# Long convolution and expert layer: the convolution in four passes of 32 channels, with the data as matmul weights in the 90-point stage and its result kept in SBUF

## The chip, the core and the metric

One core of one Trainium2 chip runs the whole program. The metric is the device time of one execution in microseconds (us). TensorE is called PE, VectorE DVE, ScalarE ACT, GpSimd POOL; SP is the engine whose queue issues nearly all DMA transfers of this kernel.

## The reference

A batch of 4 sequences of 12,480 positions and 128 channels is multiplied by a second input, convolved along the sequence with a filter that a small MLP makes, gated, and sent through a two-layer expert with a squared ReLU. All of it is float32.

```python
h_filt = (np.maximum(pos_emb @ w1, 0.0) @ w2) * np.exp(-0.01 * pos)[:, None]
u = x * v
Uf = np.fft.rfft(u, n=2 * S, axis=1)
Hf = np.fft.rfft(h_filt, n=2 * S, axis=0)
y = np.fft.irfft(Uf * Hf[None], n=2 * S, axis=1)[:, :S, :]
t = (x * y).reshape(B * S, D)
r = np.maximum(t @ w_in, 0.0)          # 128 -> 2048
out = (r * r) @ w_out                  # 2048 -> 128
```

## The kernel before

The sequence is folded into 98 rows by 128 points. The convolution is done by matmuls with constant tables in three stages, the third of which also runs the expert.

**90-point stage** (lines 110 to 302, `conv_moe`). A group g holds four of the 128 points (two and their mirror images), all 4 batches and 128 channels. `load1` brings x and v (98 rows), `u_mul` multiplies them (one half on DVE, one on POOL, line 151), `u_eo` makes sums and differences of the mirrored points (line 159). `s1_u` multiplies with the table `e_sb` as weights: 98 rows in, 90 frequencies out, 512 moving columns, cosine and sine (line 186). ACT copies the PSUM tile to `stage` (line 195) and SP stores it to the DRAM buffer `bd` (line 213). The filter goes beside it, one group of four points at a time: `pt` is loaded, `mlp1` and `mlp2` make the filter values `ft` (lines 141, 143, 168, 170), `f_eo` their sums and differences `feo` on POOL (line 181), `s1_f` transforms and stores them too (line 208). `weights` splits a piece of the expert's weights, given as 64-bit floats, into a high and a low part straight into the SBUF tiles `wi` and `wo` (lines 250 to 270). The loop over 32 groups in line 284 sets the order on every engine by hand. The stores of the last two groups are held back in part (`late`).

**128-point stage** (lines 333 to 400). For each of the 90 frequencies k, `load2` reads a row of `bd` as `bt` (128 points by 1280 columns: data and filter) and its table `wt`. `s2` transforms the filter (line 352, 256 columns) and the data (line 357, two products of 512). DVE multiplies the two spectra (`t`, line 361), POOL adds the parts (`y`, lines 369 and 370). `i2` transforms back two rows later (line 377), ACT and DVE join the halves (`ci`, `cs`, lines 379 to 382), and SP stores the row to the DRAM buffer `cd` (line 383).

**Third stage** (lines 405 to 522). For each of the 128 points, `ca` and `cb` are read from `cd`, transformed back over the 90 frequencies (`psy`, line 434), multiplied by x, transposed, and sent through the expert in blocks of 1024 tokens (lines 461 to 493).

SP issues its DMAs strictly in the order of the program: one that waits for data holds up all that follow it. Each engine, too, takes its instructions in order.

Of the kernel before, what the change touches and what calls it, by code (L numbers as in the profile page):

```python
# [29 lines left out]
F32 = mybir.dt.float32  # L31
# [9 lines left out]
FO = 64  # L41
DFF = 2048
# [12 lines left out]
ROW = 2 * W + 2 * D  # L55
RF = -(-int(np.count_nonzero(np.exp(-0.01 * np.arange(S, dtype=np.float32)))) // N2)

TERMS = ((0, 0), (1, 0), (0, 1))


def _group(n2):

    j = n2 - H2 if n2 >= H2 else H2 - 1 - n2
    return j // 2, j % 2 + (0 if n2 >= H2 else 2)
# [8 lines left out]
def conv_moe(ctx, tc, xg, vg, pos, win, w1, w2, ew, fw, ident_d, sw, iw, iw0, w_in, w_out, out):  # L73
# [11 lines left out]
    bd = dram.tile([N1, N2 + 1, ROW], F32, tag="bd", name="bd")  # L85
# [5 lines left out]
    f_sb = const.tile([N2, 2, N2], F32, tag="f", name="f_sb")  # L91
    sp.dma_start(f_sb, fw)
    ident = const.tile([R1, R1], F32, tag="id", name="ident")
    sp.dma_start(ident, ident_d)
    win_sb = const.tile([RF, N2], F32, tag="win", name="win_sb")
    sp.dma_start(win_sb, win)
# [4 lines left out]
    wi = [const.tile([D, DFF], F32R, tag=f"wi{i}", name=f"wi{i}") for i in range(2)]  # L101
    wo = [const.tile([128, NF, D], F32R, tag=f"wo{i}", name=f"wo{i}") for i in range(2)]
# [3 lines left out]
    KL = 16  # L106
    late = {NG - 2: [], NG - 1: []}
    late_pool = ctx.enter_context(ExitStack())
    lp = late_pool.enter_context(tc.tile_pool(name="late", bufs=2, side="right"))
    with ExitStack() as c1:  # L110
        io = c1.enter_context(tc.tile_pool(name="p1io", bufs=2))
        wk = c1.enter_context(tc.tile_pool(name="p1wk", bufs=2))
        psS = c1.enter_context(tc.tile_pool(name="p1s", bufs=3, space=PSUM))
        psM = c1.enter_context(tc.tile_pool(name="p1m", bufs=1, space=PSUM))
        st, sf = {}, {}

        def load1(g):
            if g >= NG:
                return
            xt = io.tile([R1, 2, 2 * W], F32, tag="x", name="xt", bufs=3)  # L120
            vt = io.tile([R1, 2, 2 * W], F32, tag="v", name="vt")
            for t, src in ((xt, xg), (vt, vg)) if g else ():
                sp.dma_start(t, src[g].rearrange("n (h w) -> n h w", h=2))
# [12 lines left out]
        def mlp1(g):  # L136
            if g >= NG:
                return
# [7 lines left out]
        def u_mul(g):  # L146
            if g >= NG:
                return
# [485 lines left out]
```

## Time and profile before

| what | value |
|---|---|
| median of 3 runs | 3200.69 us (3195.69 to 3206.71) |
| the profiled execution, its own time | 3198.17 us |
| its span, first to last instruction | 3196.2 us |
| busy share of the span | PE 96%, DVE 76%, ACT 65%, POOL 26% |
| DMA | 370.57 MB, 153956 packets, mean 116 GB/s |

A row of a group of instructions gives line, engine, operation, output and inputs with their shapes, and how many there are; then the busy time in us and the mean of one in ns; then the idle time just ahead of them and what ended it. In the order of time a row begins with its start and its duration in us, and names the idle time ahead of it in brackets. Matmuls are pipelined, and the duration of one reaches past the start of the next; how many a stretch can hold is read from the distance of two starts. A row of a stretch of time has, for each engine, busy time and the count of instructions; then the mean clock granted to TensorE, the mean busy share of the 16 DMA engines, and GB/s.

### The profile page before, as it was taken

What the parts mean: (1) busy time and instruction counts of PE and PEld (TensorE: products, weight loads), DVE (VectorE), ACT (ScalarE), POOL (GpSimd) and SP (SyncE); (2) the same over time, 40 slices, a digit from 0 to 9 for tenths busy, and PEclk for the clock granted to TensorE, in tenths of its full rate; (3) what the DMA queues carried; (4) which work ended last, traced back from release to release, by engine and by line L of the source; (5) the groups of instructions that cost most, each with busy time, mean ns of one, the idle gap of its engine ahead of it and who ended that gap; (6) DMA issues with size and microseconds to landing.
All of it is one profiled execution on the core that took longest, in us unless ns stands there. A gap on an engine that the chain in (4) does not pass through costs nothing.

```text
span 3196.2 us, 35767 instructions
## 1 busy us (share of the span) xinstructions
PE 3078.8 (96%) x12558; PEld 2239.7 (70%) x12558; DVE 2423.3 (76%) x2832; ACT 2074.8 (65%) x2453; POOL 815.7 (26%) x593
## 2 busy tenths in 40 slices
PE   8999859999699999999999999999999999999999
PEld 3343324444388888888888888888888888888888
DVE  6787738888477777777777777777777777777776
ACT  4444402222277777777777777877777777777777
POOL 3344326666212112122121211211211121121210
PEclk9999979999799999999999999999999999999999
DMA  8999749889512122112122222212221112211200
GB/s 273 307 312 308 254 153 305 297 300 296 176 51 62 54 72 58 58 52 72 55 62 58 62 61 66 58 51 59 71 59 58 58 51 74 62 53 58 63 24 19
DMA packets 153956, 370.57 MB, mean 116 GB/s; under 512 B 14841, under 2 KB 44397, under 8 KB 147701
## 3 DMA queue, kind: packets, MB, share of 16 engines
q1 hardware_dynamic: 144417, 341.80, 33.5%
q0 software_dynamic: 9360, 26.50, 3.2%
q8 instruction: 99, 1.62, 0.2%
q14 instruction: 80, 0.66, 0.1%
HBM read 236.51 MB, written 131.73 MB: 115 GB/s over the span
## 4 chain that ended last, share of the span: by engine, by line
PE 82%; DMA 13%; DVE 2%; issue 1%; SPq 1%; ACT 0%; DVEq 0%; ACTq 0%
PE psh L461 34%; PE pso L487 33%; DMA vt<-in_v_dram 9%; PE psy L434 5%; PE psx L357 4%; PE psc L377 4%; DMA wt<-in_sw_dram 3%; PE pst L449 1%; PE psh L352 1%; PE pss L186 1%; DMA cb<-cd 0%; DVE cv L252 0%; DVE u L159 0%; SPq L383 0%; DVE xt L151 0%
## 5 line engine op out<-in xcount | busy, mean ns | idle before, releaser
L81 DVE TENSOR_TENSOR glo<-gt,ghi 128x1024 fp32r<-128x1024 f32 (+1 forms) x784 | 1087.5, 1387 | 60.8 <-DVE ghi L473 1.8
L464 ACT ACTIVATE rt<-psh 128x1024 f32<-128x1024 f32 (+1 forms) x784 | 801.8, 1023 | 387.4 <-PE psh L461 373.0
L473 DVE CAST ghi<-gt 128x1024 fp32r<-128x1024 f32 (+1 forms) x784 | 540.0, 689 | 456.1 <-ACT gt L471 453.9
L487 PE MATMUL pso<-ghi,wo 128*128 128x512 f32 (+1 forms) x3136 | 852.2, 388 | 0.0
L461 PE MATMUL psh<-xhi,wi 128*128 128x512 f32 (+1 forms) x3136 | 852.2, 393 | 0.0
L471 ACT ACTIVATE gt<-rt 128x1024 f32<-128x1024 f32 (+1 forms) x784 | 828.9, 1057 | 23.4
L487 PEld LDWEIGHTS pso<-ghi,wo 128*128 128x128 f32 x3136 | 587.8, 188 | 121.5 <-DVE os L492 0.6
L461 PEld LDWEIGHTS psh<-xhi,wi 128*128 128x128 f32 x3136 | 580.1, 188 | 117.5 <-ACT rt L464 0.4
L81 POOL TENSOR_TENSOR clo<-ca,chi 128x512 fp32r<-128x512 f32 x124 | 227.2, 1833 | 1337.0 <-ACT chi L78 1294.2
L487 PE MATMUL pso<-glo,wo 128*128 128x512 f32 (+1 forms) x1568 | 497.8, 388 | 0.0
L461 PE MATMUL psh<-xlo,wi 128*128 128x512 f32 (+1 forms) x1568 | 482.4, 389 | 0.0
L461 PEld LDWEIGHTS psh<-xlo,wi 128*128 128x128 f32 x1568 | 294.7, 188 | 62.4
L487 PEld LDWEIGHTS pso<-glo,wo 128*128 128x128 f32 x1568 | 294.2, 188 | 60.9 <-DVE glo L81 0.3
L361 DVE TENSOR_TENSOR t<-psx,hs 128x1024 f32<-128x1024 f32 x180 | 212.0, 1220 | 103.1 <-PE psx L357 85.9
L186 PE MATMUL pss<-u,e_sb 98*90 98x512 f32 x512 | 247.7, 629 | 14.5 <-DVE u L159 14.4
L379 ACT COPY ci<-psc 128x512 f32<-128x512 f32 x90 | 52.8, 586 | 297.5 <-issue 203.6
L195 ACT COPY stage<-pss 90x1024 f32<-90x1024 f32 x128 | 127.5, 1007 | 100.0 <-PE pss L186 51.4
L81 POOL TENSOR_TENSOR clo<-cb,chi 104x512 fp32r<-104x512 f32 x124 | 163.4, 1317 | 104.1 <-ACT chi L78 103.6
L186 PEld LDWEIGHTS pss<-u,e_sb 98*90 98x90 f32 x512 | 79.5, 165 | 150.5 <-issue 126.0
L377 PE MATMUL psc<-y,f_sb 128*128 128x512 f32 x360 | 176.7, 613 | 5.1 <-DVE cs L382 4.5
L357 PE MATMUL psx<-bt,wt 128*128 128x512 f32 x360 | 178.2, 619 | 0.0
L369 POOL TENSOR_TENSOR y<-t,t 128x512 f32<-128x512 f32 x90 | 114.7, 1274 | 217.5 <-DVE t L361 176.6
(64 smaller groups left out, 2209.1 us busy)
## 6 DMA issues: line engine op xcount, KB each, us to landing
bt<-bd SPq DMA_DIRECT2D x90, 640.0 KB
cd<-cs SPq DMA_DIRECT2D x90, 512.0 KB
bd<-stage SPq DMA_DIRECT2D x60, 720.0 KB
cb<-cd SPq DMA_DIRECT2D x126, 208.0 KB
iwt<-in_iw_dram POOLq DMA_DIRECT2D x64, 392.0 KB, 3.5
x<-in_x_dram SPq DMA_DIRECT2D x128, 196.0 KB
out_dram<-os SPq DMA_DIRECT2D x48, 512.0 KB
xt<-in_x_dram SPq DMA_DIRECT2D x31, 784.0 KB
```

Of the source, the lines that this page charges most:

```text
L81: eng.tensor_tensor(dst, src, hi.bitcast(F32), op=ALU.subtract)
L186: pe.matmul(ps[:, c], lhsT=e_sb[: u.shape[0], e + c], rhs=u, start=True, stop=True)
L195: act.copy(s["stage"][:, e, j].rearrange("p (c w) -> p c w", c=2), ps)
L357: pe.matmul(xp[:, c], lhsT=s["w"], rhs=s["b"][:, c * W : (c + 1) * W], start=True, stop=True)
L361: dve.tensor_tensor(tt, xp.rearrange("p c (b d) -> p (c b) d", b=B), s["h"][:, c : c + 1].broadcast_to([N2, 2 * B, D]), op=ALU.mult,)
L377: pe.matmul(cp[:, c], lhsT=f_sb[:, c], rhs=s["y"][:, c], start=True, stop=True)
L434: pe.matmul(yp, lhsT=lhs, rhs=rhs, start=n == 0, stop=n == len(ops) - 1)
L461: pe.matmul(ps[:, j, :n], lhsT=wi[wp][:, f * 128 : (f + 1) * 128], rhs=bl[b][dp][:, j * n : (j + 1) * n], start=(wp, dp) == TERMS[0], stop ...
L464: act.activation(rt, ps[:, :, :n], AF.Relu)
L471: act.activation(gt, rt, AF.Square)
L473: dve.tensor_copy(hi, gt)
L487: pe.matmul(un["o"][j], lhsT=wo[tm[0]][:, f], rhs=g[tm[1]][:, j], start=f == 0 and tm == TERMS[0], stop=f == NF - 1 and tm == TERMS[-1])
```

## The change

**Four passes.** The 128 channels are taken in four passes of 32 (`Q = 4`). Within a pass the 90-point and the 128-point stage follow each other; the result of the first, for all 90 frequencies, stays in one SBUF tile `P` with a single buffer. The DRAM buffer `bd` is gone. `cd` is written in pieces of 128 columns (512 bytes) where a row had 512.

**90-point stage.** A pass has 20 chunks of 8 columns: 16 of data (batch by channel) and 4 of filter. Of a data chunk, `load_c` brings x and v in one tile `xv` (three buffers), POOL multiplies all of it, DVE makes sums and differences in `u` (three buffers). In `s1_quad` the data is now the weights of the product, and the constant table `e_sb` is what moves: for each column two products of 98 rows, 64 weight columns (the sums fill PSUM partitions 0 to 63, the differences 64 to 127) and 180 moving columns. ACT copies four columns at a time into `P`.

**Filter.** All 32 groups are computed in the first 11 chunks of pass 0, three to a chunk, and stored to a DRAM buffer `fd`; the filter chunks of every pass read from it, 8 channels (32 bytes) at a time, and DVE or POOL reorders them.

**Expert weights.** They are split in 16 pieces of 256 columns, one begun at every fourth chunk as long as the pass has some left, its work spread over three chunks, and stored to the DRAM buffer `wd`; the SBUF tiles `wi` and `wo` are filled from there in the last pass.

**128-point stage.** One step `z` takes three frequencies of 32 channels (6 products of 160 columns, then `i2` with two of 384), 30 steps a pass.

The third stage has the same instructions. x is read from a copy in another order, and the first pair of points is loaded whole when the stage begins, its x and its table earlier.

The core of the diff:

```diff
-        def s1(ps, e, u):
-            for c in range(2):
-                pe.matmul(ps[:, c], lhsT=e_sb[: u.shape[0], e + c], rhs=u, start=True, stop=True)
...
-            sp.dma_start(bd[:rows, n2, : 2 * W], src[:rows])
...
+        def filt2(g):
+            h1 = sf.pop(("h", g))
+            ps = psM.tile([RF, G2, D], F32, tag="m2", name="psm2")
+            for j in range(G2):
+                pe.matmul(ps[:, j], lhsT=h1[:, j], rhs=w2_sb, start=True, stop=True)
...
+            for e, op in enumerate((ALU.add, ALU.subtract)):
+                pool.tensor_tensor(fe[:, e], ft[:, :2], ft[:, 2:], op=op)
+            sp.dma_start(fd[:, :, 2 * g : 2 * g + 2], fe)
...
+        def load_c(g):
...
+            xv = s1.tile([R1, 2, 8 * N2], F32, tag="xv", name="xv")
+            if c < NU:
+                for r in (slice(0, 96), slice(96, R1)):
+                    sp.dma_start(xv[r], xvg[q, c][r])
+            else:
+                d = q * QC + 8 * (c - NU)
+                sp.dma_start(xv[:RF, 0].rearrange("n (m s) -> n m s", s=8),
+                             fd.rearrange("n e j d -> n (e j) d")[:, :, d : d + 8])
...
+            if c < NU:
+                pool.tensor_tensor(xv[:, 0], xv[:, 0], xv[:, 1], op=ALU.mult)
+                xr = xv[:, 0].rearrange("n (h s j) -> n h s j", h=2, s=8)
+                for e, op in enumerate((ALU.add, ALU.subtract)):
+                    dve.tensor_tensor(u[:, :, e * H2 : (e + 1) * H2], xr[:, 0], xr[:, 1], op=op)
+            else:
+                (dve, pool)[c % 2].tensor_copy(u[:RF], xv[:RF, 0].rearrange("n (m s) -> n s m", s=8))
...
+            for a in range(4):
+                for e in range(2):
+                    p = slice(e * H2, (e + 1) * H2)
+                    pe.matmul(pv[p, a], lhsT=u[:rows, 4 * h + a, p],
+                              rhs=e_sb[:rows, e : e + 2].rearrange("n c k -> n (c k)"), start=True, stop=True)
+            s = 8 * c + 4 * h
+            act.copy(
+                sl["P"][:, :, s : s + 4].rearrange("p m a t -> p a m t"),
+                pv.rearrange("p a (m t) -> p a m t", t=2),
+            )
...
+            sp.dma_start(wd[i // NWP, :, :, cols].rearrange("h p c -> p h c"), st.bitcast(F32))
...
+                for c in range(NC):
+                    g = q * NC + c
+                    load_c(g + 3)
+                    for f in range(3 * c, min(3 * c + 3, NG)) if q == 0 else ():
+                        load_f(f + 2)
+                        if f + 1 < NG:
+                            filt(f + 1)
+                        filt2(f)
+                    prep(g + 2)
+                    if c % 4 == 0 and wpart < (q + 1) * 2 * NWP // Q:
+                        part = weights(wpart)
+                        wpart += 1
+                    if part and next(part, 1):
+                        part = None
+                    s1_quad(g, 0)
+                    s1_quad(g, 1)
```

**How the order moves.** On PE, in the 90-point stage of before, a group is eight products of 512 columns (a row with `x2` stands for two), the filter's transform (`feo`), and the MLP's products (`psm`):

```order
L186 MATMUL pss_221<-u_181,e_sb 90x512 x2
L186 MATMUL pss_241<-u_181,e_sb 90x512 x2
L186 MATMUL pss_247<-feo,e_sb 90x256 x4
L168 MATMUL psm_259<-w_sb,h_209 82x128 x4
L186 MATMUL pss_269<-u_183,e_sb 90x512 x2
L186 MATMUL pss_276<-u_183,e_sb 90x512 x2
L141 MATMUL psm_281<-pt,w_sb 64x328
```

On PE in the first pass after the change, one chunk of data (`pss`, line 185) follows three MLP groups (lines 128 and 137):

```order
L128 MATMUL psm_872<-pt,w_sb 64x384
L137 MATMUL psm_876<-w_sb,h_827 96x128 x4
L128 MATMUL psm_889<-pt,w_sb 64x384
L137 MATMUL psm_893<-w_sb,h_874 96x128 x4
L128 MATMUL psm_906<-pt,w_sb 64x384
L137 MATMUL psm_910<-w_sb,h_891 96x128 x4
L185 MATMUL pss<-e_sb,u 64x180 x16
```

Three MLP groups now stand ahead of each chunk's products, and each of the latter has 180 moving columns in place of 512.

On SP, a group of before has the loads of pt, x, v and a piece of raw weights, and the stores to bd:

```order
L133 DMA pt<-in_pos_dram 64x328
L123 DMA xt<-in_x_dram 98x2048
L123 DMA vt<-in_v_dram 98x2048
L237 DMA raw<-in_w_in_dram 128x256
L213 DMA bd<-stage 90x2x1024
L208 DMA bd<-fstage 90x2x256 x2
L213 DMA bd<-stage 90x2x1024
```

On SP in the first pass after the change (`wst` is a finished piece of weights, `feo` the filter's sums and differences):

```order
L232 DMA wd<-wst 128x2x256
L155 DMA xv<-in_xv_dram 96x2048
L155 DMA xv<-in_xv_dram 2x2048
L123 DMA pt<-in_pos_dram 64x384
L145 DMA fd<-feo 192x1x256
L123 DMA pt<-in_pos_dram 64x384
L145 DMA fd<-feo 192x1x256
```

Each load of pt now stands behind the store of an earlier group's feo, and the loads of xv behind the store of a piece of weights.

On SP at the end of the second pass's 90-point stage (the rows with `xv<-fd` are the filter chunks):

```order
L155 DMA xv<-in_xv_dram 96x2048
L155 DMA xv<-in_xv_dram 2x2048
L210 DMA raw<-in_w_in_dram 128x512
L158 DMA xv<-fd 96x128x8 x2
L232 DMA wd<-wst 128x2x256
L158 DMA xv<-fd 96x128x8 x2
```

The loads from fd are new; before had no access in runs of eight elements.

More of the change, by code (lines that the diff above doesn't have):

```diff
@@ new lines, in conv_moe, with load_f, filt @@
+    win_sb = const.tile([RF, N2], F32, tag="win", name="win_sb")
+    sp.dma_start(win_sb, win)
+    f_sb = const.tile([N2, 2, N2], F32, tag="f", name="f_sb")
+    ident = const.tile([R1, R1], F32, tag="id", name="ident")
+    with ExitStack() as c1:
+        big = c1.enter_context(tc.tile_pool(name="big", bufs=1))
+        right = ExitStack()
+        s1 = right.enter_context(tc.tile_pool(name="s1", bufs=3, side="right"))
+        psX = c1.enter_context(tc.tile_pool(name="psx", bufs=2, space=PSUM))
+        pro = ExitStack()
+        wf = pro.enter_context(tc.tile_pool(name="filter", bufs=2))
+        psM = pro.enter_context(tc.tile_pool(name="psm", bufs=2, space=PSUM))
+        ch, sf, sl = {}, {}, {}
+        def load_f(g):
+            if g < NG:
+                pt = wf.tile([FO, G2 * RF], F32, tag="pos", name="pt")
+                sp.dma_start(pt, pos[g])
+                sf[g] = pt
+        def filt(g):
+            ps = psM.tile([FO, G2 * RF], F32, tag="m1", name="psm1", bufs=1)
+            pe.matmul(ps, lhsT=w1_sb, rhs=sf.pop(g), start=True, stop=True)
+            h1 = wf.tile([FO, G2, RF], F32, tag="h1", name="h1")
+            act.activation(h1.rearrange("p a b -> p (a b)"), ps, AF.Relu)
+            sf["h", g] = h1
+        def filt2(g):
+            h1 = sf.pop(("h", g))
@@ new lines, in s1_quad @@
+        def s1_quad(g, h):
+            c = g % NC
+            u, rows = ch["u", g], R1 if c < NU else RF
+            ps = psX.tile([N2, 2, 512], F32, tag="x", name="pss")
+            pv = ps.rearrange("p c (a w) -> p (c a) w", a=2)[:, :, : 2 * N1]
+            for a in range(4):
[4 more added lines that the diff above has]
+            s = 8 * c + 4 * h
@@ L265, in weights_end @@
-        def weights_end():
-            if pending:
-                hi, lo, fm, fr = pending.pop()
+                yield
+                wl, wh = raw[:, :, 0], raw[:, :, 1]
+                t, sg, m, rest = (s1.tile([128, CW], U32, tag=f"cv{n}", name=f"cv{n}", bufs=1) for n in range(4))
+                shl, shr = ALU.logical_shift_left, ALU.logical_shift_right
+                dve.tensor_scalar(t, wh, 1, 21, op0=shl, op1=shr)
+                ti = t.bitcast(I32)
+                dve.tensor_scalar(ti, ti, 896, 0, op0=ALU.subtract, op1=ALU.max)
@@ new lines, in conv_moe, with load3 @@
+    io3 = ctx.enter_context(tc.tile_pool(name="p3io", bufs=2))
+    def load3(p):
+        if p not in st3:
+            load3_w(p)
+        ca = io3.tile([128, 2, W], F32, tag="ca", name="ca")
+        cb = io3.tile([2 * CB, 2, W], F32, tag="cb", name="cb")
+        re, im = (cd[p + h * H2].rearrange("(c k) w -> k c w", c=2) for h in range(2))
+        M = 128 - N1
+        sp.dma_start(ca[:N1], re)
+        sp.dma_start(ca[N1:], im[:M])
+        for q in range(2):
+            sp.dma_start(cb[q * CB : (q + 1) * CB], im[M:])
+        st3[p].update(ca=ca, cb=cb)
```

410 lines of the change are left out of this document (153 added, 257 removed).

## Prediction

> **What bounds the kernel now.** I read the page, then busy time by stage, then the order of time inside each stage. The chain that ended last is mostly TensorE, but that is an average over three stages:
>
> ```profile
> span 3196.2 us, 35767 instructions
> PE 82%; DMA 13%; DVE 2%; issue 1%; SPq 1%; ACT 0%; DVEq 0%; ACTq 0%
> ```
>
> By stage (columns: stretch, its length, busy time of PE, PEld, DVE, ACT, POOL, then granted clock, DMA share, GB/s):
>
> ```profile
> 0.00:394.00 394.00, 357.98 (x1088) 154.92 (x1088) 306.10 (x544) 178.85 (x225) 158.11 (x100) 0.97 0.90 293
> 394.00:475.00 81.00, 39.96 (x75) 18.79 (x76) 24.77 (x26) 6.35 (x15) 17.46 (x14) 0.75 0.45 153
> 475.00:840.00 365.00, 342.92 (x827) 150.26 (x825) 301.99 (x335) 73.62 (x167) 208.41 (x167) 0.98 0.85 284
> 840.00:872.00 32.00, 17.76 (x51) 11.60 (x52) 10.21 (x17) 6.96 (x14) 2.71 (x5) 0.56 0.80 202
> 872.00:3196.20 2324.20, 2320.20 (x10521) 1904.12 (x10519) 1780.23 (x1911) 1809.00 (x2034) 429.04 (x308) 1.00 0.20 57
> ```
>
> The last 2324 us are the third stage, which the change leaves alone: PE has no gap there. What can move is what lies ahead of 840 us. The 90-point stage (to 394) waits for memory: DMA is 90% busy and the chain steps from load to load, one per group of four points.
>
> ```profile
> 175.77 12.21 DMA vt<-in_v_dram
> 188.06 11.18 DMA vt<-in_v_dram
> ```
>
> The 128-point stage steps once per row k, here from one psc to the next. PE, DVE and DMA are all nearly full in it. It ends with the last cs at 839.5 us:
>
> ```profile
> 522.11 1.95 PE L377 MATMUL psc<-y,f_sb 128*128 128x512 f32 x4
> 522.26 2.36 DVE L361 TENSOR_TENSOR t<-psx,hs 128x1024 f32<-128x1024 f32 x2 [0.29 <-PE psx L357]
> ...
> 524.76 0.69 DVE L381 TENSOR_TENSOR cs<-psc,ci 128x512 f32<-128x512 f32 x1
> ...
> 525.37 0.68 DVE L382 TENSOR_TENSOR cs<-psc,ci 128x512 f32<-128x512 f32 x1
> 526.20 1.10 PE L377 MATMUL psc<-y,f_sb 128*128 128x512 f32 x2
> ```
> ```profile
> 838.79 0.69 DVE cs L382
> ```
>
> So the convolution costs 839.5 us now. I cost the new one from zero against that.
>
> **What goes.** The round trip through bd (90 reads of 640 KB, and as many bytes written before them), and the 81 us hand-over between the stages (the second stretch above), where SP sat in single DMA issues:
>
> ```profile
> bt<-bd SPq DMA_DIRECT2D x90, 640.0 KB
> ```
> ```profile
> 427.07 10.42 SPq L383 DMA_DIRECT2D cd<-cs  x1
> ```
>
> Neither is subtracted. They are simply not in the new sum.
>
> **TensorE's price of a column.** Weight loads of one product follow each other in 0.43 us, and each fp32 product is two instructions (256 products, 512 matmuls):
>
> ```profile
> 100.20 0.16 PEld L186 LDWEIGHTS pss<-u,e_sb 98*90 98x90 f32 x1 [0.27 <-issue]
> ...
> 100.63 0.16 PEld L186 LDWEIGHTS pss<-u,e_sb 98*90 98x90 f32 x1 [0.27 <-issue]
> ```
> ```profile
> L186 PE MATMUL pss<-u,e_sb 98*90 98x512 f32 x512 | 247.7, 629 | 14.5 <-DVE u L159 14.4
> ```
>
> 0.43 / 512 is 0.84 ns a column. Swapping the operands makes the constants (180 columns) the moving side: a chunk is 16 products, 32 instructions of 180 columns, 32 x 0.151 = 4.83 us, and a pass of 20 chunks 97 us. Four passes are 387 us, where the old stage needed 256 x 0.86 = 220 us for u.
>
> **128-point stage.** A step now takes three rows of 32 channels: 12 instructions of 160 columns and 4 of 384, 12 x 0.134 + 4 x 0.323 = 2.90 us of PE. Before, a row was 2 of 256 and 8 of 512, 3.87 us, and took 4.09 (526.20 - 522.11), 1.057 times as long. DVE: 0.75 x 2.36 + 0.75 x 1.29 = 2.74 us, just hidden. At the same ratio a step is 3.07 us, 30 steps 92 us, four passes 368 us (348 with PE alone).
>
> **90-point stage, passes 1 to 3.** Rows for the work beside PE:
>
> ```profile
> L151 POOL TENSOR_TENSOR xt<-xt,vt 98x1024 f32<-98x1024 f32 x32 | 110.5, 3454 | 60.3 <-DMA vt<-in_v_dram 59.0 <-DMA xt<-in_x_dram 1.3
> L159 DVE TENSOR_TENSOR u<-xt 98x1024 f32<-98x1024 f32 x64 | 76.3, 1235 | 3.6 <-POOL xt L151 3.6
> L195 ACT COPY stage<-pss 90x1024 f32<-90x1024 f32 x128 | 127.5, 1007 | 100.0 <-PE pss L186 51.4 <-issue 48.2
> L257 DVE SCALAR_TENSOR_TENSOR cv<-raw,cv 128x128 uint32<-128x128 uint32 x32 | 9.3, 292 | 1.1
> L78 ACT CAST wi<-cv 128x128 fp32r<-128x128 f32 x16 | 4.8, 298 | 33.7 <-DVE cv L258 33.7
> L270 DVE SCALAR_TENSOR_TENSOR wi<-cv,cv 128x128 fp32r<-128x128 f32 x16 | 15.4, 965 | 0.6
> ```
> ```profile
> 839.50 3.02 DMA cd<-cs
> ```
>
> Per chunk: load 0.80 MB at 293 GB/s 2.74 us, POOL 3.45, DVE 1.24, ACT under 2.0. All hide under 4.83 us. Two things may not.
>
> First, the weight conversion. Every fourth chunk SP waits to store wst, with the next xv loads behind it, and ACT waits to cast with the chunk's own copies behind it. The loop from one store to the next: three loads 8.2, landing 2.0 (a 512 KB store takes 3.02 us, 1.2 beyond its bytes; the first pt, below, 2.8), POOL 3.45, DVE 1.24, then at 256 columns five DVE steps of 0.42, the cast 0.42, 0.42 and 1.2. That is 18.8 us against PE's 19.3 for four chunks: even. I charge 2 us each time, 8 a pass (0 to 24).
>
> Second, the filter. Each pass ends with four loads of fd in runs of 32 bytes: 96 x 128 packets, 768 for each of 16 engines if they share evenly. No row shows such a transfer. The nearest are the 64 packets of 256 bytes of w1, the 512-byte rows of win, and one lone completion packet (each first line counts packets, each second gives their share of 16 engines):
>
> ```profile
> DMA packets 64, 0.01 MB, mean 66 GB/s; under 512 B 64, under 2 KB 64, under 8 KB 64
> q1 hardware_dynamic: 64, 0.01, 30.9%
> ```
> ```profile
> DMA packets 34, 0.02 MB, mean 42 GB/s; under 512 B 2, under 2 KB 34, under 8 KB 34
> q1 hardware_dynamic: 34, 0.02, 13.9%
> ```
> ```profile
> DMA packets 1, 0.00 MB, mean 0 GB/s; under 512 B 1, under 2 KB 1, under 8 KB 1
> q1 hardware_dynamic: 1, 0.00, 0.3%
> ```
>
> The stretches are 0.2, 0.4 and 0.2 us, so a packet took 15.5, 26 and 9.6 ns. By the clock, though, w1's four packets per engine spread over 0.2 us, about 48 ns apart. I take 14 ns, nearest to 256 bytes: 10.8 us a load (7.4 at 9.6 ns, 20 at 26, 37 at 48). The first fd load can start once chunk 10's products free u and so xv; PE needs the fourth eight chunks (38.6 us) later. Four loads, landing 2.0 and the reordering copy 1.2 are 46.4: 7.8 late. After a wait of some microseconds the granted clock was 0.50 (the column ahead of the DMA share):
>
> ```profile
> 435.00:440.00 5.00, 0.49 (x1) 0.50 (x2) 0.00 (x0) 0.00 (x0) 0.00 (x0) 0.50 0.38 140
> ```
>
> so I add 3 us of slower products (0 to 5). Together 11 (0 at 9.6 ns, 113 at 48). A pass: 97 + 8 + 11 = 116.
>
> By the Trainium skill, VectorE: DVE Perf Modes, The three transpose paths, a plain DMA that transposes by strides is 19 times slower than the 1309 ns of a 128x128 one: 24.9 us for 16,384 elements, by my estimate from that page 24 ns a packet on 16 engines, 18.4 us a load and 120 us more in all. No run here shows it yet; w1's row is lower.
>
> **90-point stage, pass 0.** The 32 filter groups now go three to a chunk, and SP must store a group's feo before it can load the next pt:
>
> ```profile
> 103.31 1.10 PE L168 MATMUL psm<-w_sb,h 64*82 64x128 f32 x8
> ```
> ```profile
> L170 DVE TENSOR_TENSOR ft<-psm,win_sb 82x512 f32<-82x512 f32 x32 | 21.8, 680 | 0.0
> L181 POOL TENSOR_TENSOR feo<-ft 82x256 f32<-82x256 f32 x64 | 47.4, 761 | 168.9 <-DVE ft L170 168.9
> ```
> ```profile
> 3.67 0.60 SPq L133 DMA_DIRECT2D pt<-in_pos_dram  x1
> ...
> 6.47 1.32 PE L141 MATMUL psm<-pt,w_sb 64*64 64x328 f32 x2 [6.47 <-DMA pt<-in_pos_dram]
> ```
>
> Chain of a chunk: m1 product 0.65, m2 1.10, ft 0.68, feo 1.52, two issues 1.0, landing 2.0, m1 0.65, m2 1.10, then the 16 products 4.83: 13.5 us, and 10.7 such chunks 144. Start 13.4 (constants 4, load 2.7, landing 2, POOL and DVE 4.7), conversions 8, the other 9.3 chunks 45, fd 11: 221 us.
>
> **Sum.** 221 + 3 x 116 + 368 + 10 (four hand-overs of 2 us while ACT and DVE fill, and the last drain 2) = 947 against 839.5: 107.5 us more. The entry to the third stage has the same lines (pair 0 is now loaded whole at its start, pair 0's x and iw earlier: -2 to +3, taken as nothing). The profiled execution took 3198.2 us, its span and 2.0 around it: 3305.7. The median is 2.5 above it, so 3308.
>
> **Rivals.** *Faster: the two halves run at once.* Products of columns 0-63 and 64-127 alternate; if they overlap, a chunk is 2.42 us of PE. Alone that gives little, for the 18.8 us loop then binds and fd is hidden less: some 12 us a pass and 21 in pass 0, 3251. If reads without the bd writes also run fast enough to free the loop, and fd costs 9.6 ns, POOL's 3.45 binds: passes of 73, pass 0 of 167, 167 + 219 + 378 = 764, so 3125. It turns faster when, with pass 0 at 167, a pass takes under 98 us. For it: bd's writes are gone. Against: nothing in the trace overlaps two products. Chance 0.22. The Trainium skill, TensorEngine Tiling (Array Packing), Key Properties, says that different tiles run weight loads and matmuls in parallel; by that rule the halves overlap, and no run here shows it yet.
>
> *About even: every unknown at its low end.* Conversions 0, fd 0, landing 1.2, the 128-point stage at 348: 194 + 291 + 358 = 843, 3204. Chance 0.12, spread 0.03, 0.05, 0.04 over faster, same, slower.
>
> *Much slower: fd at 48 ns.* Four times 105 us more: 3729. Chance 0.06.
>
> That the change would not remove the traffic is no rival: no access of bd is left in its order of instructions.
>
> **How the numbers follow.** The forecast has 0.60, all slower. Slower 0.60 + 0.04 + 0.06 = 0.70, same 0.05, faster 0.22 + 0.03 = 0.25, with 0.3% (9.6 us) as what a measurement can tell from no change. The low end, 3120, is the faster rival's; the high end, 3450, is fd at 26 ns (36 us more in each pass). Outside are the slowest rival, the far part of the faster one and a rest: 2 in 10. The forecast's own range is 3230 to 3450.
>
> **What would show it.** Right: PE busy throughout in eight alternating stretches ahead of the third stage, but for the passes' ends; weight loads of pss 0.15 us apart; xv<-fd landing some 10 us apart with PE waiting 5 to 15 us at each pass's end; chunks of 13 us in pass 0; psc steps of 3.1 us. Wrong: pss instructions overlapping, so that 16 products take near 2.5 us; passes under 98 us; or the convolution over before 840 us.

## The result, and the profile after

The changed kernel takes 3437.36 us (median of 4 runs, 3433.75 to 3439.73), the kernel before 3202.97 in the same measurement: a ratio of 1.073 (95% interval 1.071 to 1.076), 234 us more. The forecast was 3308: the sign is right, the size less than half. The profiled execution has a span of 3436.2 us, 132.5 more than the 3303.7 that the forecast's sum stands for.

The chain's shares read almost like those of before and hide the difference. The second row, the clock granted to TensorE in 40 slices of the span, in tenths, falls to 5 and 6 in the first third, where no slice of before stands under 7:

```profile
span 3436.2 us, 42081 instructions
PEclk8569879798798999999999999999999999999999
PE 81%; DMA 8%; DVE 4%; POOL 1%; SPq 1%; issue 1%; ACT 0%; DVEq 0%; POOLq 0%; ACTq 0%
```

Busy time by stage (stretch, length, PE, PEld, DVE, ACT, POOL, granted clock, DMA share, GB/s): pass 0's 90-point stage, a 128-point stage, the 90-point stage of passes 1 and 3, the entry, the third stage:

```profile
0.00:267.00 267.00, 192.64 (x960) 126.91 (x960) 64.03 (x120) 48.23 (x77) 88.53 (x87) 0.66 0.53 107
267.00:362.00 95.00, 90.05 (x474) 74.41 (x476) 80.17 (x116) 29.84 (x89) 58.92 (x59) 0.95 0.61 177
362.00:485.00 123.00, 69.63 (x641) 55.57 (x642) 52.61 (x88) 32.12 (x44) 42.91 (x21) 0.72 0.80 142
...
790.00:915.00 125.00, 71.40 (x651) 56.98 (x649) 53.51 (x89) 32.43 (x46) 42.06 (x20) 0.74 0.74 126
...
1022.00:1061.00 39.00, 17.27 (x48) 10.38 (x49) 9.86 (x17) 6.26 (x13) 1.63 (x3) 0.57 0.52 142
1061.00:3436.20 2375.20, 2371.01 (x10524) 1909.86 (x10522) 1782.88 (x1912) 1808.44 (x2036) 424.33 (x308) 1.00 0.19 56
```

Three things stand out. In the 90-point stage PE is busy for 57% of a pass, at a clock of 0.72, so it seems not to be what sets the pass (e8 below tests this). Pass 0 runs at 0.66. And the third stage, taken as left alone, is 50 us longer than the 2326 us of before, with PE full and the clock at 1.00 in both.

| term (us) | forecast | measured | more |
|---|---|---|---|
| pass 0, 90-point stage | 221 | 266 | 45 |
| passes 1 to 3, 90-point stage | 3 x 116 = 348 | 121.9 + 122.6 + 122.5 = 367 | 19 |
| 128-point stages, hand-overs, drain | 378 | 389 | 11 |
| entry (last cs, at 1022.2, to first psh, at 1060.4) | 30.5 | 38.1 | 8 |
| third stage (first psh to the end) | 2326 | 2375.8 | 50 |

**Two halves at once.** Two pieces of the chain: half a chunk at full clock, and a whole chunk ahead of psc at 479 us, at granted clock 0.50:

```profile
361.94 1.40 PE pss L185 x16
...
479.24 5.07 PE pss L185 x32
```

The second looks like the forecast's 32 x 0.151 us of serial halves. It isn't: at full clock 16 instructions go in 1.40 us, the last one's own length included (16 x 0.151 would be 2.42), and the shortest whole chunks take 2.61 us; 5.07 us is the same work at half the clock.

**The loop of a pass.** SP's waits in pass 1 (362 to 485 us), and DVE's and POOL's instructions in it:

```profile
SPq L232 <- DVE wst L231: 47.2, 4, 15.4
```
```profile
392.75 2.36 POOL L169 TENSOR_TENSOR xv<-xv 98x1024 f32<-98x1024 f32 x1 [10.94 <-DMA xv<-in_xv_dram]
...
400.68 2.34 POOL L169 TENSOR_TENSOR xv<-xv 98x1024 f32<-98x1024 f32 x1 [2.04 <-DMA xv<-in_xv_dram]
403.78 2.85 POOL L169 TENSOR_TENSOR xv<-xv 98x1024 f32<-98x1024 f32 x1 [0.76 <-DMA xv<-in_xv_dram]
```
```profile
398.67 1.29 DVE L172 TENSOR_TENSOR u<-xv 98x512 f32<-98x512 f32 x2 [2.24 <-POOL xv L169]
...
400.74 2.43 DVE L219 TENSOR_SCALAR cv<-raw 128x256 uint32<-128x256 uint32 x1
...
403.75 3.43 DVE L172 TENSOR_TENSOR u<-xv 98x512 f32<-98x512 f32 x2
```

The store of wst keeps the next loads of xv back for up to 15.4 us (total, number and longest of the waits). L219, which takes 0.29 us alone, and the second instruction of the second pair of L172 (404.35 us) began while POOL's product ran and ended 0.15 and 0.55 us behind it, 2.1 us late each: DVE and POOL took turns.

**The filter's loads.** The chain shows two of the four of pass 1; the four stand between 437.6 and 477.0 us:

```profile
437.64 15.94 DMA xv<-fd
...
459.00 18.03 DMA xv<-fd
```

**The third stage.** One group of its products after, and the same group before (count, then busy time and mean ns):

```profile
L459 PE MATMUL pso<-ghi,wo 128*128 128x512 f32 (+1 forms) x3136 | 869.9, 394 | 0.0
```
```profile
L487 PE MATMUL pso<-ghi,wo 128*128 128x512 f32 (+1 forms) x3136 | 852.2, 388 | 0.0
```

The matmuls of psh and pso stand 2% further apart (starts 231.6 ns on average instead of 226.4), while ACT's and DVE's steps take what they took.

### The profile page after: what moved, and what is told of

Same layout as the page of the kernel before. It is cut to its first block, busy times and chain, and to the rows that moved or that the text cites. A ratio compares the mean times of both kernels' runs of the same rounds, so it can differ in the third digit from the quotient of the medians.

```text
span 3436.2 us, 42081 instructions
## 1 busy us (share of the span) xinstructions
PE 3157.4 (92%) x15370; PEld 2511.7 (73%) x15370; DVE 2339.0 (68%) x2784; ACT 2082.0 (61%) x2617; POOL 877.0 (26%) x693
## 3 DMA queue, kind: packets, MB, share of 16 engines
q1 hardware_dynamic: 386576, 262.96, 30.5%
## 4 chain that ended last, share of the span: by engine, by line
PE 81%; DMA 8%; DVE 4%; POOL 1%; SPq 1%; issue 1%; ACT 0%; DVEq 0%; POOLq 0%; ACTq 0%
PE psh L433 32%; PE pso L459 32%; PE psx L250 5%; PE psy L404 5%; PE psc L275 4%; DMA xv<-fd 4%; DMA xv<-in_xv_dram 2%; DVE u L172 1%; PE pst L421 1%; PE pss L185 1%; POOL xv L169 1%; DMA pt<-in_pos_dram 1%; SPq L155 1%; DMA wt<-in_sw_dram 0%; PE psm L137 0%
## 5 line engine op out<-in xcount | busy, mean ns | idle before, releaser
L436 ACT ACTIVATE rt<-psh 128x1024 f32<-128x1024 f32 (+1 forms) x784 | 800.5, 1021 | 437.8 <-PE psh L433 428.5
L459 PE MATMUL pso<-ghi,wo 128*128 128x512 f32 (+1 forms) x3136 | 869.9, 394 | 0.0
L185 PE MATMUL pss<-e_sb,u 98*64 98x180 f32 (+1 forms) x2560 | 298.4, 403 | 179.7 <-ACT P L188 74.1
L185 PEld LDWEIGHTS pss<-e_sb,u 98*64 98x64 f32 (+1 forms) x2560 | 235.3, 178 | 240.2 <-ACT P L188 153.5
L172 DVE TENSOR_TENSOR u<-xv 98x512 f32<-98x512 f32 x128 | 104.0, 853 | 248.2 <-POOL xv L169 226.8
L250 PEld LDWEIGHTS psx<-P,wt 128*128 128x128 f32 x1440 | 215.9, 190 | 49.1 <-issue 14.4
L258 DVE TENSOR_TENSOR t<-psx,hs 128x768 f32<-128x768 f32 x240 | 218.3, 952 | 45.8 <-PE psc L275 32.9
L250 PE MATMUL psx<-P,wt 128*128 128x160 f32 x1440 | 225.0, 305 | 16.2 <-DMA wt<-in_sw_dram 6.9
L188 ACT COPY P<-pss 128x720 f32<-128x720 f32 x160 | 123.7, 783 | 187.5 <-PE pss L185 187.5
L254 ACT COPY hs<-psx 128x192 f32<-128x192 f32 x240 | 64.8, 322 | 242.4 <-PE psx L250 240.7
L169 POOL TENSOR_TENSOR xv<-xv 98x1024 f32<-98x1024 f32 x64 | 153.8, 2405 | 185.7 <-DMA xv<-in_xv_dram 176.4
```

The costliest lines, as they stand in the source:

```text
L169: pool.tensor_tensor(xv[:, 0], xv[:, 0], xv[:, 1], op=ALU.mult)
L172: dve.tensor_tensor(u[:, :, e * H2 : (e + 1) * H2], xr[:, 0], xr[:, 1], op=op)
L185: pe.matmul(pv[p, a], lhsT=u[:rows, 4 * h + a, p], rhs=e_sb[:rows, e : e + 2].rearrange("n c k -> n (c k)"), start=True, stop=True)
L250: pe.matmul(xp[:, 3 * c + i, :SIG], lhsT=wt[:, i], rhs=sl["P"][:, c * (N1 // 2) + kp, :, t], start=True, stop=True)
L258: dve.tensor_tensor(t, xp[:, :, : B * QC].rearrange("p m (b d) -> p m b d", b=B), hs[:, c].rearrange("p r k d -> p (r k) d").unsqueeze(2). ...
L436: act.activation(rt, ps[:, :, :n], AF.Relu)
```

## The experiments

Unless said otherwise each is the changed kernel with one edit. All of their times on one page; "pass 1" is its 90-point stage, "conv." the last cs, "third" the third stage. e8 leaves out half of the 90-point products and e13 the conversion, so both compute other numbers. e7, e8, e10, e11 and e12 have two runs each, the others four or more. In the runs that leave the convolution as it is (e4, e7, e9, e10, e11 and the changed kernel) its end lies between 1016.3 and 1022.2 us, so a few us there mean nothing:

| run | time | ratio to before (95%) | end of pass 0 | pass 1 | conv. | third |
|---|---|---|---|---|---|---|
| kernel before | 3203.0 | 1 | | | 839.5 | 2326.2 |
| changed kernel | 3437.4 | 1.073 (1.071 to 1.076) | 266 | 121.9 | 1022.2 | 2375.8 |
| e1_order | 3437.1 | 1.074 (1.071 to 1.078) | 266 | 125.0 | 1021.7 | 2375.8 |
| e8_full | 3429.1 | 1.072 (1.069 to 1.075) | 267 | 120.8 | 1014.9 | 2375.8 |
| e2_conv | 3415.4 | 1.067 (1.064 to 1.071) | 257 | 118.4 | 1001.3 | 2376.0 |
| e5_dve | 3402.9 | 1.064 (1.062 to 1.067) | 263 | 111.4 | 987.5 | 2376.0 |
| e13_noconv | 3368.9 | 1.054 (1.053 to 1.056) | 252 | 104.3 | 954.3 | 2375.9 |
| e3_fd | 3387.8 | 1.059 (1.055 to 1.063) | 253 | 110.9 | 968.3 | 2376.0 |
| e6_feo | 3417.9 | 1.070 (1.067 to 1.072) | 249 | 121.6 | 1001.4 | 2375.7 |
| e4_wlow | 3438.4 | 1.075 (1.071 to 1.078) | 264 | 122.6 | 1018.5 | 2375.8 |
| e7_addr | 3389.4 | 1.060 (1.057 to 1.063) | 267 | 121.7 | 1021.7 | 2326.4 |
| e9_align | 3444.6 | 1.078 (1.075 to 1.080) | 265 | 121.7 | 1016.9 | 2387.1 |
| e10_128 | 3383.7 | 1.058 (1.056 to 1.061) | 264 | 122.0 | 1020.0 | 2324.8 |
| e11_w128 | 3386.0 | 1.059 (1.056 to 1.061) | 264 | 121.4 | 1016.3 | 2326.5 |
| combo | 3231.0 | 1.011 (1.008 to 1.013) | 176 | 82.8 | 802.2 | 2387.0 |
| best | 3156.2 | 0.987 (0.986 to 0.989) | 168 | 78.3 | 783.0 | 2326.4 |
| best_order | 3153.4 | 0.987 (0.985 to 0.989) | 175 | 78.7 | 790.5 | 2324.8 |
| before + alignment (b_align) | 3196.1 | 1.000 (0.998 to 1.001) | | | 828.2 | 2325.2 |
| before + 128 bytes (e12_b128) | 3247.3 | 1.015 (1.013 to 1.018) | | | 833.9 | 2375.7 |

### Does TensorE set the passes, and are the halves serial?

```diff
-            for a in range(4):
-                for e in range(2):
+            for e in range(2):
+                for a in range(4):
```

> The changed kernel with one edit: in each half chunk the four products of the first 64 columns are issued before the four of the second (in the changed kernel the two halves alternate). Theory A (new): the two halves run side by side at full clock; in the changed kernel's trace the starts of L185 stand 0.117 and 0.037 us apart in turn, 0.153 us a pair, so a chunk of 32 instructions needs 2.44 us, and the 5.07 us that I had read as serial halves is a chunk at granted clock 0.5. Then this order makes most neighbours share a half: 0.15 us an instruction, 4.9 us a chunk at full clock, and the time rises by what the waits of the passes don't cover: 0 to 49 us a pass, +20 to +100 us in all. Theory B (the one on record): the halves are serial anyway, so the spacing at full clock is the same in both kernels and the time is within 10 us.

No change in time: theory A's 20 to 100 us did not come, and theory B had the time right, but not for its reason. The chunk at 420.2 us took 3.41 us instead of 3.16, and the shortest chunks took 3.15 instead of 2.61, where serial halves would need 4.83. So the order undoes only a part of the overlap and does not decide whether there is one. The next run does.

```diff
-                for e in range(2):
-                    p = slice(e * H2, (e + 1) * H2)
-                    pe.matmul(pv[p, a], lhsT=u[:rows, 4 * h + a, p], rhs=e_sb[:rows, e : e + 2]..., ...)
+                pe.matmul(pv[:, a], lhsT=u[:rows, 4 * h + a], rhs=e_sb[:rows, 0:2]..., ...)
```

> The changed kernel with the 90-point products made with all 128 columns of u at once and the constants of the first half alone: the second half's sums come out with the wrong constants, half of the 90-point matmuls are left out, and no matmul of the program has a stationary operand of 64 columns any more. Theory E: the third stage falls from 2375.8 to about 2327 us, spacing 227 ns. Theory D or any other: it stays. For the passes: if they are paced by loads and by DVE and POOL (theory A), the time of the convolution stays within 15 us although TensorE has half of the instructions; if TensorE set them (the prediction on record), it falls by 4 x 48 us.

Its half chunk at full clock and its whole chunk at granted clock 0.5, 8 and 16 instructions with 128 weight columns:

```profile
360.03 1.39 PE L183 MATMUL pss<-e_sb,u 98*128 98x180 f32 x8
...
476.14 5.17 PE L183 MATMUL pss<-e_sb,u 96*128 96x180 f32 x16 [2.80 <-POOL u L174]
```

One full product takes what two halves take (1.39 beside 1.40 us, 5.17 beside 5.07): the halves do run at once. And with half of these instructions gone the convolution ended 7 us earlier, not 190: their number doesn't set the passes. Theory E (a lasting state of TensorE after products of 64 columns as the cause of the slower third stage, taken up again below) falls here too: the third stage stays at 2375.8 us.

### The conversion, and POOL in DVE's way

```diff
-                split_hi(hi, fm)
+                dve.tensor_copy(hi, fm)
...
+            yield
             sp.dma_start(wd[...], ...)
```

> The changed kernel with the weight conversion taken out of the way: its cast goes to DVE instead of ACT, and its store to DRAM is issued one chunk later. Theory A (the passes are paced by a loop of loads through the SyncE queue, where the store waits for DVE up to 15.4 us, 47.2 us in pass 1, with the loads queued behind it, while ACT waits 51.3 us for the same DVE steps with the copies to P behind): passes 1 to 3 fall from 123 us to about 105, pass 0 (held by the filter) stays, in all -40 to -80 us. Theory B (PE with serial halves sets the passes, 97 us, and the conversion costs what was forecast, 8 us a pass): -32 us at most, about -10.

Measured -22 us, 9 of it in pass 0 and 3.5 in pass 1: short of theory A's 40 to 80, within theory B's 32. Where the cast and the store stand matters little in a pass; the store still waited 34.8 us in pass 1.

```diff
-                pool.tensor_tensor(xv[:, 0], xv[:, 0], xv[:, 1], op=ALU.mult)
+                dve.tensor_tensor(xv[:, 0], xv[:, 0], xv[:, 1], op=ALU.mult)
```

> The changed kernel with one word changed: the product of x and v (L169) runs on DVE instead of POOL. Theory A (the passes are paced by VectorE and GpSimd keeping each other out: in the changed kernel's trace the DVE step L219 stands from 400.74 to 403.17 us beside the POOL product from 400.68 to 403.02, 2.43 us where it takes 0.21 alone, and both products of u take 3.43 us beside the next one where they take 1.29 alone; four chunks and one conversion are then 4 x (2.35 + 1.29) + 6.5 = 21 us of one or the other, against 21 to 25 measured): with the product at 1.1 to 1.3 us on DVE four chunks take 16 us, passes 1 to 3 fall by 15 to 28 us each, and pass 0 little; in all -50 to -90 us. Theory B (the loads' own time or the store's place in the queue paces them): DVE gets more work, and the time is within 15 us.

Measured -35 us, 11 a pass: less than theory A's 50 to 90, more than B's 15. DVE does more work and the passes are shorter. Two things changed at once: no POOL product stands beside DVE's steps, and the product itself takes 1.26 us on DVE where it took 2.35 on POOL; the run doesn't separate them. The step that stretched now takes 0.29 us each time:

```profile
L219 DVE TENSOR_SCALAR cv<-raw 128x256 uint32<-128x256 uint32 x4 | 1.1, 287 | 0.0
```

```diff
-                dve.tensor_scalar(t, wh, 1, 21, op0=shl, op1=shr)
-                ...
-                dve.scalar_tensor_tensor(lo, fr, 2.0**-23, fm, op0=ALU.mult, op1=ALU.add)
+                dve.tensor_copy(hi, raw[:, :, 0])
+                dve.tensor_copy(lo, raw[:, :, 1])
```

> The changed kernel with the weight conversion left out but for two plain copies (the weights' high and low words are stored as they come, so the experts work on other numbers): thirteen of fifteen steps of L215 to L231 and one of the waits on ScalarE go, while the loads, the store to DRAM and everything else stay. Theory A (the conversion's steps stand in the loop of the passes, between POOL's product and the next load, and take 6.5 us there plus what POOL keeps them waiting): four chunks take 14.6 to 17 us instead of 21 to 25, passes 1 to 3 fall by 12 to 28 us each, pass 0 by less, in all -45 to -95 us. Theory B (as on record: 8 us a pass): -20 to -35 us. Third stage: 2375.8 us as before, since nothing moves.

Measured -69 us: 17.6, 18.5 and 16.6 in passes 1 to 3, 13.5 in pass 0. This is in theory A's range: the conversion's steps, with what they wait for, cost twice the 8 us a pass of the forecast. But four chunks still take 18.3 to 19.5 us (from one store of wst to the next; 22.7 to 25.1 in the changed kernel), not theory A's 14.6 to 17; what holds them there was not tried.

### The filter's loads

```diff
-    fd = dram.tile([RF, 2, H2, D], ...)
+    fd = dram.tile([RF, Q, 2, H2, QC], ...)
-                sp.dma_start(xv[:RF, 0].rearrange("n (m s) -> n m s", s=8), fd...[:, :, d : d + 8])
+                sp.dma_start(xv[:RF].rearrange("n a w -> n (a w)"), fd[:, q, c - NU]...)
```

> The changed kernel with the filter's intermediate in DRAM laid out by pass, so that each pass reads it in two loads with 8 KB in a row instead of four with 32 bytes in a row; the filter's stores go out in runs of 256 bytes instead of 512, and the reordering into u is done by the copies on DVE and POOL. Theory A (the loads of 32-byte runs hold the DMA engines for about 40 us at the end of each pass, 437.6 to 477 us in pass 1, and PE waits for all but the 10 us that its four chunks take): passes 1 to 3 fall by 25 to 35 us each, pass 0 by 20 to 35, in all -100 to -135 us. Theory B (as on record: only one load of 10.8 us a pass shows): -44 us.

Measured -50 us, 11 to 13 a pass: theory B, the term on record. Theory A's 100 us and more did not come, since the loads' 39 us were not idle time: from 437 to 478 us TensorE was busy for 24.2 us, on 240 of the pass's 640 instructions. Without the loads the last five chunks (160 instructions) come at the end of the pass in one piece, behind the last conversion's cast:

```profile
443.34 0.40 ACT wst L84
...
444.47 14.22 PE pss L189 x160
```

### The filter's stores in pass 0

```diff
-            sp.dma_start(fd[:, :, 2 * g : 2 * g + 2], fe)
+            pool.dma_start(fd[:, :, 2 * g : 2 * g + 2], fe)
```

> The changed kernel with one word changed: the store of the filter's sums (L145) is issued from GpSimd, which makes them, instead of SyncE. Theory A (pass 0 is paced by the round store, load of the next positions, two products, sums: SyncE waits 123.1 us for POOL's sums at L145 in the first 200 us with the loads of positions behind them, and TensorE 54.2 us for those loads): pass 0 falls from 267 us to 215 to 240, the rest stays; in all -25 to -50 us. Theory B (pass 0 is paced by TensorE at granted clock 0.5, 28 to 35 busy us in each 40): the time is within 10 us, or rises by GpSimd's time to issue 32 transfers.

Measured -20 us, 17 of it in pass 0: a little short of theory A's range, beyond theory B's 10. Behind the store's wait lay the next ones, for the products that free the positions' buffer and for wst:

```profile
SPq L123 <- PE psm L128: 68.1, 22, 7.9
SPq L232 <- DVE wst L231: 64.8, 3, 27.6
```

### Where the third stage's 50 us come from

```diff
-                    wi = [w3.tile(...) ...]
-                    wo = [w3.tile(...) ...]
...
+    low = ctx.enter_context(tc.tile_pool(name="low", bufs=1))
+    wi = [low.tile(...) ...]
+    wo = [low.tile(...) ...]
```

> The changed kernel with the expert weights at the addresses of the kernel before (20 to 53 KB of each partition instead of 182 to 215 KB), which moves the third stage's other tiles up by 32 KB; the weights are then loaded after the convolution, since their place is taken by P until then. Theory C (a matmul whose stationary operand lies at the upper end of the partition takes 2% longer: the starts of psh and pso stand 227 us/1000 apart before and 231 to 234 after, at granted clock 1.00 in both): the third stage falls from 2375 us to about 2327; the loads, late now, cost 5 to 25 us ahead of it; in all -25 to -45 us. Theory D (it is the activations' places, or something else of the third stage, such as the rearranged gx at L408): the third stage stays at 2375 us and the time rises by the 5 to 25 us of the late loads.

No change, so theory C falls. Next, on top of e4, an unused tile of 14,464 bytes puts the work tiles where they were before the change:

```diff
+        wk.tile([128, 3616], F32, tag="gap", name="gap", bufs=1)
         w0 = wk.tile([128, 2, 2, 4, R1], ...)
```

> The changed kernel with every tile that the third stage's matmuls touch at the very address that it has in the kernel before (the weights at 20 to 53 KB, xhi from 118,880, ghi from 159,840 and so on; only the inverse matrices and x stay elsewhere). Moving the weights alone changed nothing: 2375.8 us, a matmul every 231.6 ns. Theory D (the place of the moving operand, or of what ACT and DVE write beside it, makes the 2%): the third stage falls to about 2327 us, spacing 227 ns. Theory E (TensorE is in another state since it has worked with stationary operands of 64 columns in the convolution, which the kernel before never does): it stays at 2375.8 and 231.6.

The third stage is back at 2326.4 us, 226.4 ns a matmul: it is the places of the tiles. Three runs asked which property of a place:

```diff
+    const.tile([128, 40], F32, tag="pad", name="pad")
...
+        wk.tile([128, 480], F32, tag="pad3", name="pad3", bufs=1)
```

> The changed kernel with two unused tiles (160 and 1920 bytes a partition) ahead of the third stage's work tiles, so that xhi, xlo, ghi, glo and the rest start at multiples of 2048 bytes (in the changed kernel they start 1984 bytes behind one, in the kernel before 96 behind one); the weights stay at the upper end. Theory D' (after e7: what counts is how a tile lies against some boundary, so that the moving rows of 2 KB cross it or not): the third stage falls from 2375.8 us to 2326 or below, since nothing can lie better than this; if it falls below 2326, the kernel before has lost time this way as well. Theory D'' (the place in the whole partition counts, high or low): it stays at 2375.8.

> The changed kernel with an unused tile of 128 bytes ahead of the third stage's work tiles: xhi goes from 71,648 to 71,776, which is 96 bytes behind a multiple of 2048 as in the kernel before, and still some 47 KB away from the place there. Theory D': 2326 us in the third stage, spacing 226.4 ns. Theory D'': 2375.8 us and 231.6 ns.

> The kernel BEFORE, with the same two kinds of unused tiles (160 and 1792 bytes), so that its weights and its third stage's work tiles start at multiples of 2048 bytes instead of 96 behind one. Theory D' with a best place at 0: its third stage falls below 2326 us by the same amount as e9's falls below 2326 (0 to 60 us), and so does its time. Otherwise: 3199 us as without.

128 bytes were enough (e10, 2324.8 us), but a multiple of 2048 made it worse (e9, 2387.1 us), where the same alignment left the kernel before as it was. So no place of the moving operand alone decides. In `b_align` the weights had moved along: wi by 160 bytes and xhi by 1952, so that their distance stayed a multiple of 256. What the fast ones share is the distance of xhi from wi: 98,560 bytes before, 110,336 the other way in e10, both multiples of 256; 110,464 in the changed kernel, 128 off; 108,384 in e9, 96 off one way and 160 the other. Two runs tested it by moving one side alone:

```diff
+                    w3.tile([128, 32], F32, tag="padw", name="padw", bufs=1)
```

> The changed kernel with only the expert weights moved, by 128 bytes (wi from 182,112 to 181,984 and so on), by an unused tile behind them; every other tile stays. Theory G (what counts is the distance of the stationary operand from the moving one: it is a multiple of 256 bytes in the kernel before, e7, e10 and the aligned kernel before, 128 off in the changed kernel and e4, 160 off in e9): the third stage falls from 2375.8 us to about 2325, spacing 226 ns. Theory H (the moving operand's place against something else that stayed, ACT's and DVE's buffers or the small constants): it stays at 2375.8 and 231.6. (The text on e9 and e10 on record gives 1984 bytes for xhi's place in the changed kernel; 71,648 is 2016 behind a multiple of 2048.)

> The kernel BEFORE with an unused tile of 128 bytes ahead of the third stage's work tiles, so that xhi, ghi and the rest lie 128 bytes off a multiple of 256 from the weights. Theory G: its third stage rises from 2326 us to about 2375, its time from 3197 to about 3246. Theory H: by e9 and the aligned kernel before, no simple place of the moving operand alone decides, and nothing is to be expected: 3197.

The group that was shown above, in e11 and in e12:

```profile
L460 PE MATMUL pso<-ghi,wo 128*128 128x512 f32 (+1 forms) x3136 | 852.2, 388 | 0.0
```
```profile
L488 PE MATMUL pso<-ghi,wo 128*128 128x512 f32 (+1 forms) x3136 | 869.9, 394 | 0.0
```

With the weights moved by 128 bytes the changed kernel is as fast there as the one before, and the kernel before, its work tiles moved by 128 bytes, as slow as the changed one. So the distance between weights and work tiles decides, as theory G says, for the distances tried (0, 128 and 160 bytes beyond a multiple of 256). All work tiles always moved together; that it is the moving operand among them, and not what ACT and DVE read and write, was not tried alone. The traces speak for it: matmuls of the changed kernel start 232.0 ns apart while ACT is idle and 232.3 while DVE is idle, those of before 227.9 and 227.3. Why the distance matters stays open.

### All together

`combo` is e3, e5, e6, the cast of e2, the conversion's store issued from POOL, and e9. `best` has e10's place instead of e9's, and the filter's copies all on DVE; `best_order` adds e1's order.

> The changed kernel with what the experiments point to, all together: the filter's intermediate by pass (e3), the product on DVE (e5), the filter's stores issued from GpSimd (e6), the cast of the conversion on DVE (half of e2) with its store issued from GpSimd as well, and the third stage's tiles at multiples of 2048 bytes (e9). Alone they gave -50, -35, -20, -22 and, by e7, -49 us. Theory A (the passes are a loop of load, VectorE and store, without the 32-byte loads and without GpSimd in VectorE's way): VectorE has 16 x 2.5 us of products and sums, 4 x 5.6 of conversion and some 5 of filter copies in a pass, 68 us, so passes 1 to 3 fall from 123 to 70 to 85 us, pass 0 from 267 to 200 to 225; convolution over at 800 to 860 us, time 3150 to 3210, about that of the kernel before. Theory B (their parts overlap: each removes the same wait): passes at 100 us or more, time above 3250.

> The kernel with all of the convolution's edits together (combo) with two things changed: the third stage's tiles 128 bytes further on, as in e10, instead of at multiples of 2048 bytes, and the filter's copies all on DVE, so that none waits in GpSimd's queue behind the store of the last conversion (there GpSimd issued that store at 336 us and made its copies to 339.9, and TensorE had 10.2 us of products left). Theory G: third stage 2325 us instead of 2375; the copies save 0 to 4 us a pass; in all 3231 - 50 - 0 to 16: 3165 to 3185, faster than the kernel before by 0.4 to 1%. Rival: the third stage's 2% has yet another condition that this layout of the program brings back, 3215 to 3235.

> The same with the order of e1: the four products of one half ahead of the four of the other. In the changed kernel that order cost nothing while TensorE waited two thirds of the passes. Theory A (the two halves overlap, and TensorE still has slack, 66 of 83 us busy in a pass): +0 to +25 us. Theory B2 (with the waits gone TensorE's share sets the passes): +18 us a pass, about +70.

The passes of `combo` are in theory A's range (82.8 us) and its pass 0 is shorter than forecast (176 us), but its time is above the 3150 to 3210: with e9's places the third stage takes 2387.0 us. Its convolution is 220 us shorter than the changed kernel's, where e2, e3, e5 and e6 alone gave 21, 54, 35 and 21, 131 in all. A likely reason is that each alone left the others' waits in place; but `combo` also has the conversion's store on POOL, which had no run of its own, so what the other 89 us are made of is not known. `best` has theory G's third stage and a time below the 3165 to 3185 forecast; it beats both kernels, by 1.3% and 8.2%. Its pass 0, its pass 1 and its third stage:

```profile
0.00:169.00 169.00, 137.90 (x960) 96.89 (x960) 95.86 (x147) 48.16 (x73) 78.79 (x104) 0.88 0.65 169
264.00:343.00 79.00, 64.73 (x642) 56.29 (x642) 62.58 (x114) 31.36 (x40) 6.43 (x7) 0.87 0.88 219
...
822.00:3147.90 2325.90, 2321.71 (x10524) 1905.29 (x10522) 1780.06 (x1912) 1809.28 (x2036) 428.93 (x308) 1.00 0.20 58
```

Now DMA is the fullest of a pass (0.88). `best_order` took 3153.4 us against 3156.2: the order of the halves still costs nothing, as theory A said.

## Why the prediction was wrong, point by point

**"The last 2324 us are the third stage, which the change leaves alone" failed: 50 us of the 132.5 that were missing.** The change takes the weights and the work tiles to other addresses, whose distance is 128 bytes off a multiple of 256; the instructions are the same, and the matmuls follow each other 2% more slowly (e7, e10, e11, e12). Same lines are not same time where the tiles move.

**"Chain of a chunk ... 13.5 us" in pass 0 failed: 45 us.** Seven of the first nine chunks took 16.8 to 18.0 us, 17.5 on average (from the first product of one to that of the next); the two with a store of wst in them took 22.3 and 22.7. The durations came from a kernel at granted clock 0.97; here, between 80 and 120 us, the clock was 0.50 (as it was from 155 to 162 us), and the filter's products took 1.47 to 1.51 us instead of 0.65 and 1.95 instead of 1.10:

```profile
80.00:120.00 40.00, 35.21 (x136) 21.09 (x136) 7.39 (x11) 6.50 (x11) 13.38 (x15) 0.50 0.36 92
```
```profile
148.99 5.27 DMA pt<-in_pos_dram
...
157.85 1.47 PE psm L128 x2
159.31 1.95 PE psm L137 x8
161.26 2.27 PE pss L185 x13
```

Each of the two products occurs twice in that chain: 2 x 0.82 + 2 x 0.85 = 3.3 us more. The load of pt, issued right behind two loads of xv, took 5.3 us to land instead of 2.0: 3.3 us more. The chunk's own products took 2.3 us of this chain instead of 4.83: 2.6 us less. That is about the 4.0 us. It is read from the trace; the clock was not tried alone. That the store stands in this round is shown: with it on another queue pass 0 is 17 us shorter (e6). The rest of the 45 us is not shown by an edit of its own: TensorE was busy for 35.2 of the 40 us above, so at this clock its own work nearly fills the chunk.

**"A chunk is 16 products, 32 instructions of 180 columns ... 4.83 us, and a pass of 20 chunks 97 us" failed, and the pass came out near by luck.** The halves overlap (e8), so TensorE needs about half of that at full clock (2.61 us in the shortest chunks). The rival that said so was right on this point, and so was the Trainium skill, TensorEngine Tiling (Array Packing), Key Properties: different tiles run their matmuls in parallel. That the pass is yet 122 us, near the forecast's 116, is the doing of the loop and of the filter's loads, which were to add only 19 us to TensorE's 97.

**"That is 18.8 us against PE's 19.3 for four chunks: even. I charge 2 us each time, 8 a pass" failed.** The loop was named, but it takes 22.7 to 25.1 us for four chunks (from one store of wst to the next), against 18.8, whose terms add up to 19.0. Without the conversion a pass is 17 us shorter (e13). What the sum lacked is that DVE and POOL take turns: it let other chunks' POOL products run beside DVE's steps at no cost. From the landing of the loads to the next store it had 8.8 us (3.45 + 1.24 + five of 0.42 + 0.42 + 0.42 + 1.2); in this turn of the loop it was 13.6:

```profile
411.75 9.32 DMA xv<-in_xv_dram
...
421.22 2.36 POOL xv L169
423.61 1.29 DVE u L172 x2
...
426.13 2.29 issue
...
428.70 3.35 DVE u L172 x2
...
434.33 0.43 DVE wst L231
```

The 2.29 us and the 2.1 us by which the second pair is late are DVE behind POOL's products of the next two chunks (425.9 and 428.5 us). With the product on DVE a pass is 11 us shorter (e5), a part of which is DVE's shorter product. The Trainium skill, SBUF — State Buffer, Who interferes with whom, says it: a DVE instruction with two inputs in SBUF, or in a mode that takes both ports, and a GpSimd instruction that reads SBUF keep each other out for their whole length. The trace agrees (L219 from 0.29 to 2.43 us beside POOL's product).

**"I take 14 ns", 11 us a pass, held.** Four loads took 39.4 us (437.6 to 477.0), 49,152 packets on 16 engines: 12.8 ns each. Removing them gave 11 to 13 us a pass (e3). The 24 ns that I had estimated from the Trainium skill, VectorE: DVE Perf Modes, The three transpose paths, was too much: the page speaks of transposing copies with a large innermost stride at the destination, and this load writes runs of eight elements one behind the other. The measurement decides.

**The range.** 3437 us lies inside 3230 to 3450 by luck: the high end stood for loads of fd at 26 ns a packet, and these took 12.8. What brought the time there were the third stage and pass 0, with 95 us together.

**The 128-point stage** held: 2.98 us a step (psx starts at 284.46, 287.44 and 290.42) for 3.07. The last of its four stages took 6 to 8 us longer than the others, beside the loads of weights and x, and hand-overs were 3 to 6 us for 2. **The entry**, "-2 to +3, taken as nothing", was 8 us longer, 6 of them ahead of the first psy, which began 15.5 us behind the last cs (1037.8) instead of 9.2 (848.7): pair 0, now loaded whole behind the last store, waits for its loads, of which this one stands on the chain:

```profile
1026.62 12.40 DMA cb<-cd
```

## What to carry to other kernels

A stage that is left alone in the code can still change when the tiles around it move: compare its time in both traces before anything else, and look at the distance between the weights and the tiles they work on when matmuls follow each other more slowly by a few per cent at the same clock. Sum a loop over the queue that closes it (load, the steps on DVE and POOL in turn, store, next load), and count steps of DVE and POOL that both read SBUF one behind the other. Read the granted clock beside every duration that a sum takes over from another stage. Where several waits stand in one loop, an edit alone may show little of its worth: four parts here gave 131 us one by one and 220 together, with one more edit that was not tried alone.

## What the hardware showed that was not expected

- Matmuls of 512 float32r columns start 226.2 to 226.4 ns apart when the work tiles (the moving operand among them) lie a multiple of 256 bytes from the stationary operand, 231.6 at 128 bytes beyond such a multiple and 233.0 at 160 bytes beyond (e9), at granted clock 1.00; 2.1 to 2.6% of a third stage of 2326 us.
- Two products with 64 weight columns each into different halves of PSUM's partitions took the time of one with 128 (1.40 and 1.39 us for half a chunk).
- The chunk of two halves took 5.07 us at granted clock 0.50, which can't be told from serial halves at full clock by its length alone: the clock has to be read beside it.
